# Triangular systems of four chunks solved together on VectorE, one to a partition, in an RWKV-7 recurrence with a tanh-shrink layer

## The chip, the cores and the metric

The kernel runs on one core of a Trainium2 chip. The metric is device time in microseconds (us) of one execution, and a version's time is the median of its runs. The engines named below are TensorE (PE, with PEld its weight loads), VectorE (DVE), ScalarE (ACT), GpSimd (POOL) and SyncE (SP), which issues the DMAs. Each engine takes its instructions in the order in which they were written for it.

## The reference

```python
# r, k, v, w, a, b: (4, 8, 768, 40); w lies in 0.85 .. 0.95; w_in: (320, 2048), w_out: (2048, 320)
for t in range(S):
    y[:, :, t] = np.einsum('bhd,bhde->bhe', rt, state)
    Sa = np.einsum('bhde,bhe->bhd', state, at)
    state_decay = state * wt[:, :, None, :] - np.einsum('bhd,bhe->bhde', Sa, bt)
    state = state_decay + np.einsum('bhd,bhe->bhde', vt, kt)
x = y.transpose(0, 2, 1, 3).reshape(3072, 320)
h = x @ w_in
return (h - np.tanh(h)) @ w_out
```

Everything is float32, but for the two weights, which come as float64 and are taken apart into float32 on the chip.

## The kernel before

The 768 tokens are cut into 24 chunks of 32. One chunk covers all 4 batches and 8 heads: a tile of 128 partitions holds 4 x 32 tokens, and matrices over tokens are block diagonal. Heads go in pairs, each head's 40 channels on 64 partitions. Within a chunk the recurrence is a unit lower triangular system of 32 x 32 for each batch and head, (I + N) U = -(A V + A S0), where S0 is the state that enters the chunk.

`prep(c)` does what needs no state. It loads k, b, a, r, v as `x_t`, takes the running products of the decays (`pr`, a scan), their reciprocals (`rp`), scales k, b and a, turns four of these to tokens on partitions (`p_nat`, `nat`), and forms the products (`p_prod`) of b with a (`m`, and the first `z`) and of k with a (`at`). Then comes the inverse: block sizes 2, 4, 8, 16, for each half of the heads, each a transpose (`p_flip`, line 246), a product with m (`p_g`, masked on VectorE at line 280 into `g`) and a product with z (`p_z`, subtracted on VectorE at line 285). It ends with `u0`, the inverse times `av`, and `w_`, the inverse times a (`p_w`).

`chain(c)` does what needs the state `st`: `p_u` = w times st, `ub` and `vb` (u and v spread over the batches), the new state (`p_st`), the transposes `p_s` of the old state and `p_ut` of u, the products `rv` and `ru`, the output `p_y` and `y`, and the transposes `p_x` that hand 128 tokens to the layer.

The layer runs for 256 tokens, that is, after every second chunk. It is a generator of ten pieces: eight pairs of rows of `p_h` = w_in times x with tanh and its series (ACT, POOL and DVE), then two outputs `p_o`. A call of `tick()` issues one piece. Before the change there are five ticks a chunk, four between the steps of the inverse and one in `chain`, so the ten pieces spread over two chunks. The weights are loaded and converted in 40 pieces through the scratch tiles `raw`, `wt`, `wf` (lines 159 to 174), 20 after chunk 0 and the rest after chunk 1. A scheduler sets the final order on each engine from the order of the code, so pieces of neighbouring steps interleave. All PSUM results but the layer's share five banks (`bank`); the layer has three of its own.

Of the kernel before, what the change touches and what calls it, by code (L numbers as in the profile page):

```python
# [53 lines left out]
def rwkv_shrink(ctx: ExitStack, tc: tile.TileContext, r, k, v, w, a, b, tok, dec, chan, w_in, w_out, out):  # L54
# [10 lines left out]
    assert B * L == P and DP >= D and H % 2 == 0 and NCH % 2 == 0  # L65
# [10 lines left out]
    un = chunks.enter_context(tc.tile_pool(name="un", bufs=2))  # L76
# [18 lines left out]
    # before[s, t] = 1 where s < t in one batch  # L95
# [4 lines left out]
    # pair_t[s, t] = -1 where s and t = s + 1 are a block of two  # L100
    pair_t = fixed("pair_t", [P, P], BF16)
    G.memset(pair_t, 0.0)
    v_ = pair_t.rearrange("p (j q) -> p j q", q=2)[:, :, 1]
    G.memset(v_, -1.0)
    keep(v_, Alu.is_equal, [[-2, P // 2]], 0, 1)
    # join[h][t, s] = 1 where t is in the second and s in the first half of one block of 2 h
    join = {}
    h = 2
    while h < L:
        m_ = join[h] = fixed(f"join{h}", [P, P], BF16)  # L110
        G.memset(m_, 0.0)
        v_ = m_.rearrange("p (j q) -> p j q", q=2 * h)[:, :, 0:h]
        G.memset(v_, 1.0)
        keep(v_, Alu.is_ge, [[-2 * h, P // (2 * h)], [0, h]], -h, 1)
        keep(v_, Alu.is_ge, [[2 * h, P // (2 * h)], [0, h]], 2 * h - 1, -1)
        h *= 2
    # own[p, b] = 1 where partition p is a token of batch b
# [4 lines left out]
    # half[p, e] = 1 where partition p is a channel of the pair's head e  # L122
# [4 lines left out]
    # what the scan of the decays adds: 1 before each batch's first token  # L127
# [5 lines left out]
    # of each chunk: the greatest and the least product of decays; 0, or NaN if an output isn't finite  # L133
# [6 lines left out]
    # the state, transposed: [(e, channel of k), batch, pair, e', channel of v], zero but for e = e'  # L140
    st = fixed("st", [P, B, HP, 2, DP])
    G.memset(st, 0.0)
    u_nat = [fixed(f"u_nat{i}", [P, H, DP]) for i in range(2)]
# [7 lines left out]

    def weight(dst, src, n):
        """A piece of a weight, [rows, n], into SBUF as float32."""
# [4 lines left out]
        # float64 bits: sign 1, exponent 11, fraction 52, low word first (and values in float32's range).  # L158
        raw = ff.tile([P, WP, 2], I32, name="raw", tag="raw", bufs=1)[:rows, :n]
        nc.sync.dma_start(out=raw, in_=src.bitcast(I32).rearrange("p (n two) -> p n two", two=2))  # L160
        lo, hi = raw[:, :, 0], raw[:, :, 1]
        t_ = ff.tile([P, WP], I32, name="wt", tag="wt", bufs=1)[:rows, :n]
        f_ = ff.tile([P, WP], I32, name="wf", tag="wf", bufs=1)[:rows, :n]
# [21 lines left out]
    todo = []  # L185
# [7 lines left out]
    def prep(c):  # L193
        g = {}
        v_n = g["v"] = io.tile([P, H, D], F32, name="v_n", tag="v_n")
        nc.sync.dma_start(out=v_n, in_=tok[c].rearrange("p (h d) -> p h d", h=H))
        w_t = io.tile([P, HP * B * E1], F32, name="w_t", tag="w_t", bufs=1)
        nc.sync.dma_start(out=w_t, in_=dec[c])
        x_t = io.tile([P, 5, HP, P], F32, name="x_t", tag="x_t", bufs=2)
        nc.sync.dma_start(out=x_t, in_=chan[c].rearrange("p (j q t) -> p j q t", j=5, q=HP))  # L200
        k_t, b_t, a_t, r_t, v_t = (x_t[:, j] for j in range(5))
        g["r_t"], g["v_t"] = r_t, v_t

        # the decays' running products: pr[..., i] is that of i tokens
        pr_ = sb.tile([P, HP * B, E1], F32, name="pr", tag="pr", bufs=2)
        V.tensor_tensor_scan(pr_.rearrange("p x i -> p (x i)"), w_t, reset.rearrange("p x i -> p (x i)"), 0.0,
                             Alu.mult, Alu.add)
        # (held to where quotients of them are sound: if one of them was not there, seen tells)
        V.tensor_scalar(pr_, pr_, PR_MAX, None, Alu.min, Alu.max, accum_out=seen[:, c, 0:1])
        V.tensor_scalar(pr_, pr_, PR_MIN, None, Alu.max, Alu.min, accum_out=seen[:, c, 1:2])  # L210
        rp = sb.tile([P, HP * B, L], F32, name="rp", tag="rp")
        V.reciprocal(rp, pr_[:, :, 1:])  # L212
        blk = lambda x: x.rearrange("p q (b t) -> p (q b) t", b=B)
        G.tensor_tensor(blk(k_t), blk(k_t), rp, Alu.mult)  # L214
        G.tensor_tensor(blk(b_t), blk(b_t), rp, Alu.mult)
        V.tensor_tensor(blk(a_t), blk(a_t), pr_[:, :, 0:L], Alu.mult)
        pe_t = rp.rearrange("p (q b) t -> p q (b t)", q=HP)
        G.tensor_copy(rp, pr_[:, :, 0:L])
        # the state's decay over the chunk, for both halves of a pair
        pc = g["pc"] = sb.tile([P, B, HP, 2], F32, name="pc", tag="pc", bufs=2)  # L220
# [3 lines left out]
        nat = sb.tile([P, 4, H, DP], F32, name="nat", tag="nat", bufs=2)  # L224
        g["k"], g["b"], g["a"], g["p"] = (nat[:, j] for j in range(4))
        for j, x in enumerate((k_t, b_t, a_t, pe_t)):
            p_ = bank("p_nat")
            for q in range(HP):
                T.transpose(p_[:, q * P:(q + 1) * P], x[:, q, :], ident)  # L229
            A.copy(nat[:, j].rearrange("p h d -> p (h d)"), p_)  # L230

        def prod(e, l_, r_):
            p_ = bank("p_prod")
            for q in range(HP):
                r0 = e * DP
                mm(p_[:, q * P:(q + 1) * P], l_[r0:r0 + D, q, :], r_[r0:r0 + D, q, :], q == 0)
            return p_.rearrange("p (q t) -> p q t", q=HP)
        g["prod"] = prod

        def unit(name, bufs=2):  # L240
            return un.tile([P, HP, P], F32, name=name, tag=name, bufs=bufs)

        def flip(src, dst):
            p_ = bank("p_flip")
            for q in range(HP):
                T.transpose(p_[:, q * P:(q + 1) * P], src[:, q, :], ident)  # L246
            A.copy(dst.rearrange("p q t -> p (q t)"), p_)  # L247

        g["z"], ats = [], []
        ms = []  # L250
        for e in range(2):
            m_ = unit("m")
            p_ = prod(e, b_t, a_t)
            A.copy(m_, p_)
            z = unit("z", 4)
# [9 lines left out]
        for h in range(H):  # L265
            mm(p_av[:, h * D:(h + 1) * D], ats[h % 2][:, h // 2, :], v_n[:, h, :], h == 0)
# [203 lines left out]
    while todo:  # L470
        tick()
# [57 lines left out]
```

## Time and profile before

| | us |
|---|---|
| median of 3 runs | 2021.6 |
| lowest and highest run | 1999.52 and 2028.64 |
| span of the profiled execution | 2022.6 |
| TensorE busy in it | 1836.2 |
| VectorE busy in it | 1133.3 |

The profile is of one execution. Its page gives the busy time of each engine, the chain of work that ended last, and the costliest groups of instructions. A group's row has the line, the engine and operation, the tile written and the tiles read, the shapes, the count, then the busy time in us and the mean duration of one in ns, then the idle time of the engine just ahead of it with what ended that idle time. Matrix products of float32 are two instructions each in the trace, transposes one. The mean duration of a matmul contains its pipeline, so the spacing of starts says more about throughput than the mean. A row of the timeline has the start and the length of a run of equal instructions. A window's row has its length, each engine's busy time with the number of instructions, the granted TensorE clock as a share of full speed, the share of the DMA engines and GB/s.

### The profile page before, as it was taken

Reading aid. Unit: us, or ns where it says so; the run is one execution under the profiler, and the core shown is the slowest. Engines: PE = TensorE matmul, PEld = TensorE weight load, DVE = VectorE, ACT = ScalarE, POOL = GpSimd, SP = SyncE. Lnnn points to the kernel's source line nnn. Section 1 sums busy time; section 2 is a strip of 40 time slices with the busy share of each in tenths; the row PEclk is TensorE's granted clock in tenths of the full one; section 3 lists DMA queues with packets and bytes.
Section 4 is the critical chain, followed back from the end, with each engine's and each line's share of the span. In section 5 each row is a group of like instructions: output and inputs, shape, how many; then the busy total and the mean of one; then the engine's idle time right before and its main releaser. Section 6 shows DMA issues by size and latency. Waiting matters only on the chain.

```text
span 2022.6 us, 28394 instructions
## 1 busy us (share of the span) xinstructions
PE 1836.2 (91%) x11978; PEld 1474.7 (73%) x11978; DVE 1133.3 (56%) x1887; ACT 478.0 (24%) x909; POOL 401.6 (20%) x400
## 2 busy tenths in 40 slices
PE   4878897889999999899899899899899899989998
PEld 4767676777777877777777777777777777777865
DVE  6577768667465375474375375366365457347333
ACT  1011221113132132231132132132122123123121
POOL 4011130103122032031032032032022122122012
PEclk9977879798897899998898998988978979889867
DMA  3111011110101001001001010010010000100000
GB/s 104 52 36 54 13 42 45 61 60 15 38 5 35 30 13 39 30 9 39 30 10 36 7 36 31 12 35 27 16 36 14 29 30 1 36 27 1 7 1 8
DMA packets 18916, 58.17 MB, mean 29 GB/s; under 512 B 1888, under 2 KB 8032, under 8 KB 15712
## 3 DMA queue, kind: packets, MB, share of 16 engines
q1 hardware_dynamic: 18784, 56.30, 8.4%
q8 instruction: 96, 1.57, 0.3%
q14 instruction: 36, 0.29, 0.0%
HBM read 52.36 MB, written 3.93 MB: 28 GB/s over the span
## 4 chain that ended last, share of the span: by engine, by line
PE 79%; DVE 12%; POOL 4%; issue 2%; ACT 2%; DMA 1%; SPq 0%; ACTq 0%; DVEq 0%; POOLq 0%
PE p_h L85 16%; PE p_o L85 11%; PE p_g L85 10%; PE p_z L85 9%; PE p_y L85 8%; PE p_flip L246 5%; PE p_st L85 4%; DVE rp L212 4%; PE p_u L85 3%; PE p_nat L229 3%; PE p_av L85 3%; PE p_prod L85 3%; PE p_s L325 2%; DVE g L280 2%; POOL z L257 2%
## 5 line engine op out<-in xcount | busy, mean ns | idle before, releaser
L85 PE MATMUL p_h<-xT,w 128*128 128x256 f32 (+1 forms) x1152 | 395.4, 461 | 2.9 <-DVE w L174 2.4
L85 PEld LDWEIGHTS p_h<-xT,w 128*128 128x128 f32 (+1 forms) x1152 | 206.1, 213 | 131.3 <-issue 116.1
L85 PE MATMUL p_o<-w,gt 128*128 128x320 f32 x768 | 278.3, 491 | 0.2 <-DVE w L174 0.2
L85 PEld LDWEIGHTS p_g<-t,m 128*128 128x128 f32 x1536 | 217.5, 212 | 80.6 <-ACT t L247 70.6
L85 PE MATMUL p_g<-t,m 128*128 128x128 f32 x1536 | 238.4, 304 | 35.4 <-ACT t L247 35.4
L85 PE MATMUL p_z<-z,g 128*128 128x128 f32 x1536 | 228.6, 296 | 45.3 <-DVE g L280 45.3
L85 PEld LDWEIGHTS p_z<-z,g 128*128 128x128 f32 x1536 | 206.6, 205 | 84.9 <-DVE g L280 77.1
L280 DVE TENSOR_TENSOR g<-p_g,join 128x512 f32<-128x512 f32 x192 | 132.1, 688 | 185.1 <-PE p_g L85 184.6
L247 ACT COPY t<-p_flip 128x512 f32<-128x512 f32 x192 | 112.5, 586 | 472.9 <-PE p_flip L246 469.8
L285 DVE TENSOR_TENSOR z<-z,p_z 128x512 f32<-128x512 f32 x192 | 131.3, 684 | 136.3 <-PE p_z L85 135.4
L329 POOL TENSOR_TENSOR vb<-v_n,own 128x1280 f32<-128x1280 f32 x23 | 53.8, 2340 | 665.1 <-PE p_st L85 665.1
L85 PEld LDWEIGHTS p_o<-w,gt 128*128 128x128 f32 x768 | 148.2, 214 | 49.6 <-issue 19.9
L246 PE MATMUL p_flip<-ident,z 128*128 128x128 f32 x768 | 132.0, 294 | 40.0 <-POOL z L257 40.0
L403 POOL TENSOR_SCALAR qu<-qu 128x512 f32<-128x512 f32 x96 | 63.3, 659 | 509.6 <-ACT qu L399 509.3
L246 PEld LDWEIGHTS p_flip<-ident,z 128*128 128x128 f32 x768 | 100.1, 156 | 42.7 <-POOL z L257 42.5
L404 POOL TENSOR_TENSOR qu<-qu,sq 128x512 f32<-128x512 f32 x96 | 126.6, 1318 | 7.9
L212 DVE RECIPROCAL rp<-pr 128x512 f32<-128x512 f32 x24 | 80.4, 3352 | 74.4 <-PE p_nat L229 74.4
L405 DVE SCALAR_TENSOR_TENSOR qu<-qu,sq 128x512 f32<-128x512 f32 x96 | 66.3, 690 | 92.4 <-POOL qu L404 92.4
L85 PE MATMUL p_prod<-x_t 40*128 40x128 f32 x1152 | 112.1, 289 | 1.7 <-DVE st L343 1.7
L397 ACT ACTIVATE th<-p_h 128x512 f32<-128x512 f32 x96 | 57.3, 597 | 229.9 <-PE p_h L85 229.5
L85 PEld LDWEIGHTS p_prod<-x_t 40*128 40x128 f32 x1152 | 102.7, 191 | 10.7 <-issue 6.2
L214 POOL TENSOR_TENSOR x_t<-x_t,rp 128x512 f32<-128x512 f32 x24 | 31.0, 1293 | 369.5 <-DVE rp L212 369.5
(267 smaller groups left out, 2461.2 us busy)
## 6 DMA issues: line engine op xcount, KB each, us to landing
x_t<-in_chan SPq DMA_DIRECT2D x24, 1280.0 KB
w_t<-in_dec SPq DMA_DIRECT2D x24, 264.0 KB
raw<-in_w_out SPq DMA_DIRECT2D x16, 320.0 KB
raw<-in_w_in SPq DMA_DIRECT2D x16, 256.0 KB
v_n<-in_tok SPq DMA_DIRECT2D x24, 160.0 KB
raw<-in_w_in SPq DMA_DIRECT2D x8, 128.0 KB
out<-o__2684 SPq DMA_DIRECT2D x1, 160.0 KB
out<-o__2746 SPq DMA_DIRECT2D x1, 160.0 KB
```

The source lines that it names most:

```text
L85: T.matmul(o, l_, r_, start=first, stop=last, skip_group_check=True)
L212: V.reciprocal(rp, pr_[:, :, 1:])
L229: T.transpose(p_[:, q * P:(q + 1) * P], x[:, q, :], ident)
L246: T.transpose(p_[:, q * P:(q + 1) * P], src[:, q, :], ident)
L247: A.copy(dst.rearrange("p q t -> p (q t)"), p_)
L280: V.tensor_tensor(gg, p_.rearrange("p (q t) -> p q t", q=HP), heads4(join[h_]), Alu.mult)
L285: V.tensor_tensor(z2.rearrange("p q t -> p (q t)"), z.rearrange("p q t -> p (q t)"), p2, Alu.subtract)
L329: G.tensor_tensor(vb, g["v"].rearrange("p h d -> p (h d)").unsqueeze(1).to_broadcast([P, B, DM]), own.unsqueeze(2).to_broadcast([P, B, DM] ...
L397: A.activation(t_, p_, Act.Tanh)
L403: G.tensor_scalar(q_, q_, -1.0, GAM, Alu.mult, Alu.add)
L404: G.tensor_tensor(q_, q_, s_, Alu.mult)
L405: V.scalar_tensor_tensor(q_, q_, C0, s_, Alu.add, Alu.mult)
```

## The change

`prep` becomes two functions. `first(c)` does the decays and the scaling, forms only the 32 x 32 blocks of b times a (`p_n`, `n_c`) and stores them in DRAM (`n_d`). When four chunks have done so, their 4 x 4 x 8 = 128 systems are loaded with one system to a partition (`nt`), and `invert` solves them by 31 steps of substitution, a multiply and a subtract each, on VectorE. The inverses go through DRAM (`z_d`) into two block diagonal tiles `z`. `second(c)` does the rest that needs no state, and `chain` applies the inverse to one right hand side, `rhs`, made of `at` times v and a times the state. The first four chunks are prepared and inverted before chunk 0. Later, the `first` calls of the next group stand after the first two chunks of a group, and `invert` is advanced two steps at each tick. Ticks now stand at twelve places in `second` and `chain`. The two halves of the heads alternate in `p_prod`. The scratch for the weights is now in the buffer of the layer's `gt`, in two turns. `y_t` (r and v) has one buffer, `n_c`, `nt`, `zt` and `nat` one, `x_t` and `rp` six.

```diff
+GR = 4
+NK = 6
...
+    space = ff.tile([P, 2, NF * P], I32, name="gt", tag="gt", bufs=1)
...
     def tick():
         while todo and next(todo[0], todo) is todo:
             todo.pop(0)
+        step()
+        step()
+    def step():
+        while subst and next(subst[0], subst) is subst:
+            subst.pop(0)
...
+    def first(c):
...
+        n_c = sb.tile([P, HP, 2, L], F32, name="n_c", tag="n_c")
+        p_e = [bank(f"p_n{e}") for e in range(2)]
+        for q in range(HP):
+            for b in range(B):
+                for e in range(2):
+                    r0, t0 = e * DP, b * L
+                    mm(p_e[e][t0:t0 + L, q * L:(q + 1) * L], b_t[r0:r0 + D, q, t0:t0 + L],
+                       a_t[r0:r0 + D, q, t0:t0 + L], q == 0)
+        for e in range(2):
+            A.copy(n_c[:, :, e, :], p_e[e][:, :HP * L].rearrange("p (q t) -> p q t", q=HP))
...
+        for b in range(B):
+            nc.sync.dma_start(out=n_d[c % GR, b].rearrange("h (s t) -> s h t", t=L),
+                              in_=n_c[b * L:(b + 1) * L].rearrange("p q e t -> p (q e) t"))
+    def invert(i_):
+        nt = sb.tile([P, L, L], F32, name="nt", tag="nt")
+        nc.sync.dma_start(out=nt.rearrange("p s t -> p (s t)"), in_=systems[i_].rearrange("c b h x -> (c b h) x"))
...
+        for j in range(L - 1):
+            k_, n_ = j + 1, L - 1 - j
...
+            V.tensor_tensor(t3, nt[:, j, j + 1:].unsqueeze(1).to_broadcast([P, k_, n_]),
+                            zt[:, 0:k_, j].unsqueeze(2).to_broadcast([P, k_, n_]), Alu.mult)
+            V.tensor_tensor(zt[:, 0:k_, j + 1:], zt[:, 0:k_, j + 1:], t3, Alu.subtract)
+            yield
+        z_d = inverses[i_] = dr.tile([GR, B, H, L * L], F32, name="z_d", tag="z_d", bufs=2)
+        nc.sync.dma_start(out=z_d.rearrange("c b h x -> (c b h) x"), in_=zf)
+        yield
+    def second(c, g):
...
+        y_t = io.tile([P, 2, HP, P], F32, name="y_t", tag="y_t", bufs=1)
...
+        for b in range(B):
+            nc.sync.dma_start(out=z[b * L:(b + 1) * L, :, b * L:(b + 1) * L],
+                              in_=inverses[c // GR][c % GR, b].rearrange("h (s t) -> s h t", t=L))
...
-        h_ = 2
-        while h_ < L:
...
     def chain(c, g, x_t):
+        p_r = bank("p_r")
+        for h in range(H):
+            mm(p_r[:, h * D:(h + 1) * D], g["at"][h % 2][:, h // 2, :], g["v"][:, h, :], h == 0)
         if c > 0:
             for q in range(HP):
                 for b in range(B):
+                    mm(p_r[b * L:(b + 1) * L, 2 * q * D:2 * (q + 1) * D], g["a_t"][:, q, b * L:(b + 1) * L],
+                       st[:, b, q, :, :D], False)
+        rhs = sb.tile([P, H, D], F32, name="rhs", tag="rhs")
+        A.activation(rhs.rearrange("p h d -> p (h d)"), p_r[:, :DM], Act.Copy, scale=-1.0)
+        p_u = bank("p_u")
+        for h in range(H):
+            mm(p_u[:, h * D:(h + 1) * D], g["z"][:, h, :], rhs[:, h, :], h == 0)
...
-    g = prep(0)
+    parts = [first(c) for c in range(GR)]
+    for _ in invert(0):
+        pass
     for c in range(NCH):
...
+        second(c, parts[c])
+        chain(c, parts[c], x_t)
+        if nxt < NCH and i_ < 2:
+            parts += [first(nxt + 2 * i_ + j) for j in range(2)]
+            if i_ == 1:
+                subst.append(invert(nxt // GR))
...
+        if i_ == GR - 1:
+            while subst:
+                step()
```

On TensorE before, the inverse of a chunk stands with the layer's `p_o` (or `p_h`) between its steps; this is the first part of one chunk:

```order
L85 MATMUL p_g<-t,m 128x128 x4
L85 MATMUL p_o<-w_132,gt 128x320 x2
L85 MATMUL p_z<-z,g 128x128 x4
L246 MATMUL p_flip<-ident,z 128x128 x4
L85 MATMUL p_o<-w_132,gt 128x320 x2
```

On TensorE now, this is the middle of an even chunk, ahead of the state's update (`p_st`):

```order
L88 MATMUL p_h<-xT,w_111 128x256 x14
L88 MATMUL p_r<-v_n,at 128x40
L88 MATMUL p_h<-xT,w_111 128x256 x3
L88 MATMUL p_r<-v_n,at 128x40 x7
L88 MATMUL p_r<-st,x_t 32x80 x16
L88 MATMUL p_h<-xT,w_111 128x256 x2
L88 MATMUL p_u<-rhs,z_103 128x40 x8
L330 MATMUL p_s<-ident,st 128x128 x16
```

And this is the same place in the odd chunk that follows:

```order
L88 MATMUL p_r<-v_n,at 128x40 x8
L88 MATMUL p_r<-st,x_t 32x80 x16
L88 MATMUL p_u<-rhs,z_104 128x40 x8
L330 MATMUL p_s<-ident,st 128x128 x16
L88 MATMUL p_st<-vb,nat 128x320
L88 MATMUL p_st<-ub,nat 128x320
```

The steps p_g, p_z and p_flip are gone, the layer's matmuls stand in runs in the even chunks, and none stand in the odd ones.

On VectorE now, the substitution (lines 256 and 258) stands between the layer's operations, here in the third chunk of a group:

```order
L406 TENSOR_TENSOR gt<-p_h,th 128x512
L256 TENSOR_TENSOR tmp<-nt,zt 128x175
L409 SCALAR_TENSOR_TENSOR qu<-qu,sq 128x512
L258 TENSOR_TENSOR zt<-zt,tmp 128x7x25
L410 TENSOR_TENSOR qu<-qu,p_h 128x512
L412 TENSOR_SCALAR mk<-sq 128x512
L256 TENSOR_TENSOR tmp<-nt,zt 128x192
```

Where g and z stood four times for each half of the heads in every chunk, two small operations now stand between two of the layer's.

On ScalarE now, at the head of the second chunk of a group, the copies `n_c` of two calls of `first` stand around the copies of `nat`; what an instruction waits for stands in brackets:

```order
L234 COPY n_c<-p_n_4134 128x4x32 [waits DMAHW5_49,DMAHW7_49,DMAHW0_49,PE_49]
L234 COPY n_c<-p_n_4135 128x4x32 [waits PE_49]
L282 COPY nat<-p_nat 128x512 [waits DVE_49,PE_49]
L282 COPY nat<-p_nat 128x512 [waits PE_49] x2
L234 COPY n_c<-p_n_4192 128x4x32 [waits DMAHW2_49,DMAHW1_49,DMAHW7_49,DMAHW0_49,Activation_49]
L234 COPY n_c<-p_n_4193 128x4x32
L316 ACTIVATE rhs<-p_r 128x320 [waits PE_49]
```

The third copy waits for DMAs that read the first two, and `rhs` stands behind it.

More of the change, by code (lines that the diff above doesn't have):

```diff
@@ L142, in rwkv_shrink @@
     G.memset(st, 0.0)
+    z_bufs = [fixed(f"z{i}", [P, H, P]) for i in range(2)]
+    for z_ in z_bufs:
+        G.memset(z_, 0.0)
     u_nat = [fixed(f"u_nat{i}", [P, H, DP]) for i in range(2)]
@@ new lines, in second @@
+    def second(c, g):
+        v_n = g["v"] = io.tile([P, H, D], F32, name="v_n", tag="v_n")
+        nc.sync.dma_start(out=v_n, in_=tok[c].rearrange("p (h d) -> p h d", h=H))
+        y_t = io.tile([P, 2, HP, P], F32, name="y_t", tag="y_t", bufs=1)
+        nc.sync.dma_start(out=y_t, in_=chan[c, :, 3 * HP * P:].rearrange("p (j q t) -> p j q t", j=2, q=HP))
+        g["r_t"], g["v_t"] = y_t[:, 0], y_t[:, 1]
+        z = g["z"] = z_bufs[c % len(z_bufs)]
+        for b in range(B):
+            nc.sync.dma_start(out=z[b * L:(b + 1) * L, :, b * L:(b + 1) * L],
+                              in_=inverses[c // GR][c % GR, b].rearrange("h (s t) -> s h t", t=L))
+        nat = sb.tile([P, 3, H, DP], F32, name="nat", tag="nat")
+        g["k"], g["b"], g["p"] = (nat[:, j] for j in range(3))
+        for j, x in enumerate((g["k_t"], g["b_t"], g["pe"])):
@@ L238, in prep @@
         g["prod"] = prod
[L240 to L255, printed above, removed]
-            V.tensor_tensor(z, p_, heads4(pair_t), Alu.mult)
-            G.tensor_tensor(z, z, heads4(ident), Alu.add)
-            ms.append(m_)
-            g["z"].append(z)
@@ L291, in prep @@
-        p_u = bank("p_u0")
-        for h in range(H):
-            mm(p_u[:, h * D:(h + 1) * D], g["z"][h % 2][:, h // 2, :], av[:, h, :], h == 0)
-        u0 = g["u0"] = sb.tile([P, DM], F32, name="u0", tag="u0", bufs=2)
-        A.copy(u0, p_u[:, :DM])
-        p_w = bank("p_w")
-        for h in range(H):
-            r0 = (h % 2) * DP
-            mm(p_w[r0:r0 + DP, (h // 2) * P:(h // 2 + 1) * P], g["a"][:, h, :], g["z"][h % 2][:, h // 2, :], h < 2)
-        w_ = g["w"] = sb.tile([P, HP, P], F32, name="w_", tag="w_", bufs=2)
@@ L301, in prep @@
-        A.activation(w_.rearrange("p q t -> p (q t)"), p_w, Act.Copy, scale=-1.0)
-        return g
+        g["at"] = []
+        for x in prod(g["k_t"], g["a_t"]):
+            at = un.tile([P, HP, P], F32, name="at", tag="gram")
+            V.tensor_tensor(at, x, heads4(before), Alu.mult)
+            g["at"].append(at)
+        tick()
     def chain(c, g, x_t):
@@ L334, in chain @@
             for q in range(HP):
+                tick()
                 p_ = bank("p_st")
@@ L351, in chain @@
         ru, rv = [], []
-        for e in range(2):
-            x = un.tile([P, HP, P], F32, name="rv", tag="rv")
-            V.tensor_tensor(x, g["prod"](e, g["v_t"], g["r_t"]), heads4(before), Alu.mult)
-            rv.append(x)
-        for e in range(2):
-            x = un.tile([P, HP, P], F32, name="ru", tag="ru")
-            V.tensor_tensor(x, g["prod"](e, u_t, g["r_t"]), heads4(before), Alu.mult)
-            ru.append(x)
+        for x_, l_, n_ in ((rv, g["v_t"], "rv"), (ru, u_t, "ru")):
+            for p_ in g["prod"](l_, g["r_t"]):
+                x = un.tile([P, HP, P], F32, name=n_, tag="gram")
+                V.tensor_tensor(x, p_, heads4(before), Alu.mult)
+                x_.append(x)
+            tick()
         for h in range(H):
```

119 lines of the change are left out of this document (42 added, 77 removed).

## Prediction

> **What bounds the kernel now.** I read the page's busy line and its chain of work that ended last, then the groups by shape, then windows with the granted clock, then the timeline of the stages that the change touches.
>
> ```profile
> PE 1836.2 (91%) x11978; PEld 1474.7 (73%) x11978; DVE 1133.3 (56%) x1887; ACT 478.0 (24%) x909; POOL 401.6 (20%) x400
> PE 79%; DVE 12%; POOL 4%; issue 2%; ACT 2%; DMA 1%; SPq 0%; ACTq 0%; DVEq 0%; POOLq 0%
> q1 hardware_dynamic: 18784, 56.30, 8.4%
> ```
>
> TensorE is busy 91% of the span and is 79% of the chain; VectorE is half idle. The transposes p_x close a chunk, so they date the chunks: these three close chunks 3, 7 and 23 (counted from 0).
>
> ```profile
> 368.45 0.90 PE L380 MATMUL p_x<-ident,y 128*128 128x128 f32 x3 [0.61 <-DVE y L370]
> 700.47 0.52 PE L380 MATMUL p_x<-ident,y 128*128 128x128 f32 x3
> 1944.47 0.90 PE L380 MATMUL p_x<-ident,y 128*128 128x128 f32 x3 [0.61 <-DVE y L370]
> ```
>
> Sixteen chunks, eight pairs, take 1244 us: 155.5 us a pair, each pair carrying one call of the layer. The windows (length, then busy us of PE, PEld, DVE, ACT, POOL, the granted clock, DMA) say what fills that:
>
> ```profile
> 700.47:1944.47 1244.00, 1164.08 (x8036) 941.62 (x8034) 658.66 (x998) 318.30 (x609) 250.38 (x233) 0.91 0.07 23
> 1944.47:2022.60 78.13, 71.22 (x165) 40.69 (x165) 24.86 (x47) 15.83 (x28) 17.58 (x16) 0.63 0.02 5
> 1945.00:1996.00 51.00, 50.54 (x98) 26.77 (x96) 20.60 (x38) 13.17 (x23) 15.35 (x14) 0.50 0.00 0
> ```
>
> Per pair TensorE works 145.5 us and idles 10. The last layer alone is a tail of 78 us, in which p_h runs at half clock although TensorE never idles. The clock matters elsewhere too; these windows cover the end of one chunk:
>
> ```profile
> 997.00:1000.40 3.40, 3.40 (x40) 3.28 (x40) 2.94 (x5) 0.45 (x1) 1.46 (x2) 1.00 0.00 0
> 1000.40:1003.80 3.40, 3.40 (x20) 3.40 (x20) 0.03 (x1) 0.00 (x0) 0.00 (x0) 0.57 0.00 0
> 1007.20:1010.60 3.40, 3.40 (x16) 3.36 (x17) 0.50 (x2) 1.70 (x4) 0.00 (x0) 0.50 0.87 319
> ```
>
> The clock falls while p_y (40 columns a matmul) keeps TensorE busy, and stays at 0.5 until the next chunk's transposes have run: some 10 us a chunk, costing about 5.
>
> **The change, part by part.** *Squaring removed from TensorE.* Its groups, and the same work at full clock in the timeline:
>
> ```profile
> L85 PE MATMUL p_g<-t,m 128*128 128x128 f32 x1536 | 238.4, 304 | 35.4 <-ACT t L247 35.4
> L85 PE MATMUL p_z<-z,g 128*128 128x128 f32 x1536 | 228.6, 296 | 45.3 <-DVE g L280 45.3
> L246 PE MATMUL p_flip<-ident,z 128*128 128x128 f32 x768 | 132.0, 294 | 40.0 <-POOL z L257 40.0
> L85 PE MATMUL p_prod<-x_t 40*128 40x128 f32 x1152 | 112.1, 289 | 1.7 <-DVE st L343 1.7
> L85 PE MATMUL p_w<-z,nat 128*64 128x128 f32 x384 | 37.6, 288 | 0.0
> 960.36 1.05 PE L85 MATMUL p_g<-t,m 128*128 128x128 f32 x8
> 961.25 1.24 PE L85 MATMUL p_o<-w,gt 128*128 128x320 f32 x4
> 962.33 1.05 PE L85 MATMUL p_z<-z,g 128*128 128x128 f32 x8
> 963.22 0.60 PE L246 MATMUL p_flip<-ident,z 128*128 128x128 f32 x4
> 963.66 1.24 PE L85 MATMUL p_o<-w,gt 128*128 128x320 f32 x4
> 1024.83 2.28 PE L85 MATMUL p_h<-xT,w 128*128 128x256 f32 x8
> 1945.83 50.52 PE L85 MATMUL p_h<-xT,w 128*128 128x256 f32 x96 [0.46 <-ACT xT L382]
> ```
>
> The groups together are 599 us, 25.0 a chunk, at the clock as it was. Start to start at full clock, p_g takes 0.89 us, p_z 0.89, p_flip 0.44: 2.2 us, eight times a chunk, 17.8 us. I take this lower figure, since groups overlap. With it go p_w (37.6/24 = 1.6), the transposes of a (0.44) and the product of b and a (16 instructions of 97 ns, 1.6). Together 21.4 us a chunk.
>
> *p_n added.* 64 instructions of 32x32 a chunk. Nearest below is p_u<-st, which also fills strips of 32 columns, 32 in 0.76 us or 24 ns each: 1.5 us. Nearest above is p_prod at 97 ns: 6.2 us. I take 2.0, as neighbours go to different strips. The other solve, p_u on rhs, and p_r on at and st replace p_u on av, p_av and p_u on w, count for count: nothing, in work. Net per pair: -2 x 19.4 = -39 us.
>
> ```profile
> 989.18 0.76 PE L85 MATMUL p_u<-st,w__6467 128*32 128x80 f32 x32 [0.69 <-ACT w__6467 L301]
> 989.87 1.97 PE L325 MATMUL p_s<-ident,st 128*128 128x128 f32 x16
> 991.35 1.49 DVE L332 TENSOR_TENSOR ub<-p_u,own 128x1280 f32<-128x1280 f32 x1 [0.77 <-ACT u_nat L317]
> L280 DVE TENSOR_TENSOR g<-p_g,join 128x512 f32<-128x512 f32 x192 | 132.1, 688 | 185.1 <-PE p_g L85 184.6
> L285 DVE TENSOR_TENSOR z<-z,p_z 128x512 f32<-128x512 f32 x192 | 131.3, 684 | 136.3 <-PE p_z L85 135.4
> L212 DVE RECIPROCAL rp<-pr 128x512 f32<-128x512 f32 x24 | 80.4, 3352 | 74.4 <-PE p_nat L229 74.4
> L206 DVE TENSOR_TENSOR_SCAN pr<-w_t,reset 128x528 f32<-128x528 f32 x24 | 47.9, 1997 | 33.2 <-POOL rp L218 24.4 <-POOL reset L130 8.8
> L209 DVE TENSOR_SCALAR_CACHE_REDUCE pr<-pr 128x528 f32<-128x528 f32 x24 | 16.8, 699 | 0.5
> L216 DVE TENSOR_TENSOR x_t<-x_t,pr 128x512 f32<-128x512 f32 x24 | 20.0, 834 | 0.0
> ```
>
> *Substitution on VectorE.* 684 ns for 512 elements and 1491 for 1280 give 146 ns plus 1.05 ns an element. A group of four chunks has 62 operations on 2 x 5456 elements: 9.1 + 11.5 = 20.5 us, six groups 123 us, against 263 us of g and z removed. VectorE gets lighter. The steps stand between the layer's operations, in the second half of each group, where it has time: nothing on the path, except that later operations of the chain wait a third of a us behind one.
>
> *The layer gathered in even chunks.* There are now 12 ticks a chunk, so all ten pieces fall in the first chunk of a pair and the odd chunk has no filler. Going through its chain: it waits for at (two operations of 0.68 plus hand-offs, 1.5 us), for rhs (0.6), and for y (0.6); ub's 1.49 is covered by the 16 transposes p_s, and u_t by the product of v and r. So 3 us of waits replace the 10 us of old idle time (mostly the squaring's own): -7 a pair.
>
> *p_n at the head of a chunk.* Two chunks of four begin with two p_n clusters. n_c has one buffer, so the second copy on ScalarE waits until four DMAs have read the first, and behind it stand rhs and, through the five banks, p_prod. Price: the copy, issue, and landing. The nearest row is this load of 1280 KB, issued at 1006.62 and over within the window ending 1010.60 above or just behind it, so 4 us for far more bytes:
>
> ```profile
> 1006.62 0.33 SPq L200 DMA_DIRECT2D x_t<-in_chan  x1
> ```
>
> 4 us twice in four chunks, from 0 (hidden) to 8: +4 a pair, and +2 for the time that chain operations queue. y_t has one buffer too, but its load has 20 us before v and r are used.
>
> *The clock.* p_r and p_u are now one run of 40-column matmuls and thin ones, like p_y; I count a second drop of the clock in each odd chunk (4 us) and a slower start of p_h in the even one (3 us): +7. Bounds: 0 to +30, as in the second rival. **A pair:** 155.5 - 39 - 7 + 6 + 7 = 122.5 us.
>
> *The alternating products.* The heads' two halves now alternate in p_prod. The row of p_u<-st shows neighbours in different column strips at 24 ns; no row shows different row strips. I take no gain, with up to 2 us a chunk at the low end. [...]
>
> *The start.* Four chunks must be prepared and a group inverted before chunk 0, and the first layer's gt waits for all weights, whose scratch is now that buffer. In VectorE's order the last weight operation stands in chunk 2. Ahead of it: nine preparations of 7.7 us (scan 2.0, two clamps of 0.7 and their read-outs, reciprocal 3.35, product 0.83) 69, the weights, 52 inversion pairs 36, chains 28.
>
> ```profile
> sum 600.00, DVE 100.62; mean DVE 16.77
> sum 600.00, DVE 64.66; mean DVE 10.78
> L164 DVE TENSOR_SCALAR wf<-raw x40: 264/294/1071, 13.8 to 438.9; 128x256 int32<-128x256 int32 x16, 128x320 int32<-128x320 int32 x16, 64x256 int32<-64x256 int32 x8
> 1996.40 19.75 PE L85 MATMUL p_o<-w,gt 128*128 128x320 f32 x64
> ```
>
> The first two are VectorE's busy time on tiles wf and raw; the third is in both, 40 of 0.3 us, so weights are about 152 us. Sum 285, from 9 us on at 90%: 325. Then eight layer tiles of about 4 us (p_h alone is 12 x 0.285 = 3.4), 64 p_o at 0.31, p_y: chunk 2 ends near 380. An odd chunk: the pair's 145.5 less 10 for the half clock less the layer at full clock (96 x 0.285 + 64 x 0.27 = 45) is 45 a chunk, less 19.4 is 26, plus 3 of waits and 9 for the clock: 38 us. So chunk 3 ends near 418, against 368 before. Bounds 370 to 450.
>
> **Sum.** 418 + ten pairs x 122.5 - 5 (chunk 23 updates no state) + the unchanged tail 78 = 1716 us. It is made against the profiled span of 2022.6 us, which is 1 us from the median of 2021.6.
>
> **Rivals.** *The clock stays up.* If only idle time dropped it, the old 10 us (two chunks of 5) and my 7 would go: 105 a pair, and p_h in the tail, 96 in 50.5 us, would take 27. 418 + 1050 - 5 + 55 = 1518. Speaking against it: the 51 us window at 0.50 with TensorE busy 50.54. 10%. [...]
>
> *The clock stays down.* In even chunks some 70 p_h instructions now stand together before p_r, without the p_g and p_z that ran between them. If they run as in the tail (0.526 us) rather than at 0.285, a pair pays 17 more, and up to 8 more if the odd chunk stays down: 140 to 148, so 1891 to 1971. For it: that window. Against: transposes still stand between. 18%.
>
> *The small DMAs become the bound.* n_d and z move 2 x 1024 pieces of 128 bytes a chunk, 128 per DMA engine. The queue line gives 0.084 x 16 x 2022.6 / 18784 = 145 ns a packet: 19 us a chunk, hidden. From 0.6 us a piece (77 us) they are longer than a chunk was; at 0.7 the kernel takes 24 x 90 = 2150. Nothing in the profile shows pieces that slow. 4%. *The inverse comes late* is milder: each of five groups would have to be 60 us late to cancel the gain.
>
> **How the numbers follow.** My forecast 68%, clock up 10%, clock down 18%, small DMAs 4%. The forecast's own width is 1590 to 1830 (start +-40, p_n and DMA waits +-40, clock +-60). The range 1540 to 1900 takes in half of each clock rival and leaves out 18%. Runs before spread over 1.4%, so 2% is about what can be told from no change. Faster by over 2% (below 1981): the forecast, clock up, nearly all of clock down: 0.93; within 2%: 0.03; slower: 0.04.
>
> **What would show it.** p_flip, p_g, p_z gone; TensorE busy near 1250 us; 62 operations a group at 0.18 to 0.42 us; odd chunks 32 to 45 us and even ones 75 to 95; chunk 3 ending at 380 to 450. Wrong if p_r or p_u waits for z in steady chunks, if p_h is at 0.5 through whole even chunks, or if ScalarE waits over 8 us at n_c.

## The result and the profile after

The changed kernel takes 1586.5 us (median of four runs, 1565.8 to 1596.4) against 2012.9 us for the kernel before (four runs, 1999.5 to 2028.6). The ratio is 0.781, with a 95% interval of 0.773 to 0.789. The forecast was 1716 us in a range of 1540 to 1900. The ratio is that of the faster runs, for the changed kernel 1565.8 and 1577.0 us (mean 1571.4); the other two took 1596 us, the profiled execution (1596.0 us, span 1594.3) among them, so its durations are compared with each other below and small differences between two kernels are not read from it.

The page of the changed kernel: busy time of the engines, the chain that ended last, and the DMA queue.

```profile
PE 1356.3 (85%) x8810; PEld 1021.4 (64%) x8810; DVE 932.1 (58%) x1804; ACT 315.9 (20%) x645; POOL 356.8 (22%) x347
PE 65%; DVE 26%; POOL 3%; issue 2%; ACT 2%; DMA 1%; SPq 0%; ACTq 0%; DVEq 0%; POOLq 0%
q1 hardware_dynamic: 76192, 68.90, 15.4%
```

TensorE has 3168 matmul instructions fewer and is still the bound, but VectorE's part of the chain has doubled. The queue moves four times the packets in 15.4% of its time, that is 52 ns a packet (0.154 x 16 x 1594.3 / 76192): the small pieces are hidden.

Windows of the changed kernel, up to the end of chunk 3, to the end of chunk 23, and the tail (length, busy us of PE, PEld, DVE, ACT, POOL, clock, DMA):

```profile
359.73:1516.05 1156.32, 1087.83 (x7149) 825.31 (x7149) 624.95 (x1092) 261.32 (x532) 261.45 (x240) 0.77 0.13 35
1516.05:1594.30 78.25, 71.06 (x165) 40.60 (x165) 24.96 (x47) 15.83 (x28) 17.57 (x16) 0.63 0.02 5
```

Chunk 3 ends at 359.7 us instead of 368.5, ten pairs take 115.6 us each instead of 157.6 (1944.47 less 368.45, by ten), and the tail is unchanged. So nearly all of the gain lies in the steady pairs. This is the same stretch of the kernel before:

```profile
368.45:1944.47 1576.02, 1478.12 (x10081) 1192.91 (x10081) 853.56 (x1329) 398.50 (x762) 316.91 (x293) 0.90 0.08 25
```

A pair loses 39.0 us of TensorE's busy time (147.8 less 108.8) and 2.9 us of its idle time (9.8 less 6.9), although the granted clock fell from 0.90 to 0.77. Two even chunks in the same place of their groups, chunk 8 and chunk 12, are the most telling rows of this profile:

```profile
600.30:691.29 90.99, 90.24 (x387) 62.99 (x387) 41.76 (x66) 20.26 (x38) 22.40 (x21) 0.69 0.09 25
844.36:912.44 68.08, 66.80 (x388) 47.87 (x388) 44.22 (x66) 19.82 (x38) 22.69 (x21) 0.95 0.12 33
```

The same instructions in the same order took 91.0 us in one and 68.1 in the other. TensorE is busy throughout both; the granted clock is 0.69 in one and 0.95 in the other. Their timelines, at the same place, show where:

```profile
607.99 1.11 PE L281 MATMUL p_nat<-ident,x_t 128*128 128x128 f32 x4
608.90 6.22 PE L88 MATMUL p_h<-xT,w 128*128 128x256 f32 x12
615.05 1.12 PE L281 MATMUL p_nat<-ident,rp 128*128 128x128 f32 x4
...
850.48 0.66 PE L281 MATMUL p_nat<-ident,x_t 128*128 128x128 f32 x4
850.97 3.34 PE L88 MATMUL p_h<-xT,w 128*128 128x256 f32 x12
```

Twelve p_h take 6.2 us or 3.3. Where the clock was down when p_h began, p_h did not soon bring it up again: of the ten steady even chunks four (6, 8, 14 and 16) took 91 to 98 us at a clock of 0.67 to 0.69, with 72 to 74 of their 96 p_h at half clock; six took 67 to 79 at 0.89 or more, with 18 or fewer.

The odd chunks were to have 3 us of waits. This is chunk 5, TensorE and VectorE, and the window of the chunk (an idle time and what ended it stand in brackets):

```profile
432.63 1.41 PE L88 MATMUL p_prod<-x_t 40*128 40x128 f32 x16
436.74 3.75 PE L88 MATMUL p_r<-v_n,at 128*128 128x40 f32 x16 [2.70 <-issue]
442.28 3.64 PE L88 MATMUL p_u<-rhs,z 128*128 128x40 f32 x16 [0.56 <-ACT rhs L316]
457.68 0.41 PE L88 MATMUL p_y<-nat,rv 128*128 128x40 f32 x2 [1.57 <-DVE rv L361]
...
432.74 3.35 DVE L213 RECIPROCAL rp<-pr 128x512 f32<-128x512 f32 x1 [4.39 <-PE p_nat L281]
436.01 1.22 DVE L298 TENSOR_TENSOR at<-p_prod,before 128x512 f32<-128x512 f32 x2
```

The windows of the whole chunk and of the 14 us from the idle time on:

```profile
427.81:465.65 37.84, 32.21 (x356) 28.84 (x356) 16.09 (x26) 6.21 (x16) 5.64 (x5) 0.68 0.22 58
434.00:448.00 14.00, 10.75 (x76) 10.29 (x76) 4.72 (x4) 1.97 (x6) 1.78 (x2) 0.56 0.30 84
```

TensorE idles 5.6 us of 37.8. The longest wait, 2.7 us ahead of p_r, has no releaser in its row ("issue"), but the times tell it: p_r begins as the first half of `at` is done, and before `at` on VectorE stands the reciprocal that `first` does for a later chunk, 3.35 us long. The clock is 0.56 over these 14 us, and p_r, p_u and p_s run at half speed (p_u takes 3.64 us, against 1.98 in chunk 10 at full clock).

### The profile page after: what moved, and what is told of

The parts are those of the page before. It is cut to its first block, busy times and chain, and to the rows that moved or that the text cites. A ratio compares the mean times of both kernels' runs of the same rounds, so it can differ in the third digit from the quotient of the medians.

```text
span 1594.3 us, 21763 instructions
## 1 busy us (share of the span) xinstructions
PE 1356.3 (85%) x8810; PEld 1021.4 (64%) x8810; DVE 932.1 (58%) x1804; ACT 315.9 (20%) x645; POOL 356.8 (22%) x347
## 2 busy tenths in 40 slices
DMA packets 76297, 70.34 MB, mean 44 GB/s; under 512 B 54688, under 2 KB 60832, under 8 KB 76192
## 3 DMA queue, kind: packets, MB, share of 16 engines
q1 hardware_dynamic: 76192, 68.90, 15.4%
## 4 chain that ended last, share of the span: by engine, by line
PE 65%; DVE 26%; POOL 3%; issue 2%; ACT 2%; DMA 1%; SPq 0%; ACTq 0%; DVEq 0%; POOLq 0%
PE p_h L88 21%; PE p_o L88 9%; PE p_y L88 9%; PE p_r L88 5%; PE p_st L88 5%; PE p_u L88 4%; PE p_s L330 4%; DVE tmp L256 3%; DVE zt L258 3%; PE p_nat L281 3%; DVE rp L213 3%; PE p_prod L88 2%; DVE rv L361 2%; DVE pr L207 1%; PE p_x L384 1%
## 5 line engine op out<-in xcount | busy, mean ns | idle before, releaser
L88 PE MATMUL p_o<-w,gt 128*128 128x320 f32 x768 | 216.7, 441 | 2.7 <-DVE gt L413 2.7
L406 DVE TENSOR_TENSOR gt<-p_h,th 128x512 f32<-128x512 f32 x96 | 65.6, 684 | 120.3 <-ACT sq L402 120.3
L88 PE MATMUL p_u<-rhs,z 128*128 128x40 f32 x384 | 76.8, 382 | 56.2 <-DMA z<-z_d 47.3
L88 PEld LDWEIGHTS p_u<-rhs,z 128*128 128x128 f32 x384 | 75.3, 298 | 61.7 <-issue 47.4
L88 PE MATMUL p_r<-v_n,at 128*128 128x40 f32 x384 | 76.7, 368 | 39.0 <-issue 32.0
L88 PEld LDWEIGHTS p_r<-v_n,at 128*128 128x128 f32 x384 | 74.0, 283 | 48.4 <-issue 38.3
L334 POOL TENSOR_TENSOR vb<-v_n,own 128x1280 f32<-128x1280 f32 x23 | 54.7, 2377 | 180.0 <-PE p_st L88 98.1
L88 PE MATMUL p_y<-nat,rv 128*128 128x40 f32 x384 | 62.3, 319 | 38.4 <-DVE rv L361 36.9
L88 PEld LDWEIGHTS p_y<-nat,rv 128*128 128x128 f32 x384 | 56.3, 226 | 45.2 <-DVE rv L361 44.0
L413 DVE COPY_PREDICATED gt<-mk,qu 128x512 f32<-128x512 uint8 x96 | 84.6, 881 | 0.4
L256 DVE TENSOR_TENSOR tmp<-nt,zt 128x31 f32<-128x31 f32 (+15 forms) x186 | 74.4, 400 | 1.9
```

The source lines that it names most:

```text
L88: T.matmul(o, l_, r_, start=first, stop=last, skip_group_check=True)
L256: V.tensor_tensor(t3, nt[:, j, j + 1:].unsqueeze(1).to_broadcast([P, k_, n_]), zt[:, 0:k_, j].unsqueeze(2).to_broadcast([P, k_, n_]), Alu. ...
L334: G.tensor_tensor(vb, g["v"].rearrange("p h d -> p (h d)").unsqueeze(1).to_broadcast([P, B, DM]), own.unsqueeze(2).to_broadcast([P, B, DM] ...
L406: V.tensor_tensor(o_, p_, t_, Alu.subtract)
L413: V.copy_predicated(o_, m_, q_)
```

## The experiments

**The clock.** From the trace of the changed kernel I added up, for each stretch of 3.41 us (the 71 changes of the granted clock in this trace lie whole multiples of 3.41 us apart), the time in which columns stream, weighted by the rows and columns of the array that a matmul uses. A column takes about 1.7 ns at half clock (16 p_s of 128 columns in chunk 5: 0.216 us each) and half that at full clock (0.111 us each in chunk 10). Of 35 rises 32 followed a stretch with 0.75 or more of the array at work; of 185 stretches that stayed down 184 had less; all 36 falls followed stretches below 0.38, and no stretch that stayed up had less. My estimate from this one trace is that the clock goes by the share of the array at work. How long TensorE is busy does not tell it: in the tail 96 p_h, one after the other, took 50.5 us, all at a clock of 0.50. Four kernels test what counts as work. The first fills the third piece of the contraction, 64 channels, with zeros to 128:

```diff
+    xts = [fixed(f"xT{i}", [P, len(KT), 2 * P]) for i in range(2)]
+    for t_ in (w1, *xts):
+        G.memset(t_[KT[-1][1]:, len(KT) - 1, :], 0.0)
...
-                    mm(p_[:, i * 2 * P:(i + 1) * 2 * P], w1[:n, k_, (f + i) * P:(f + i + 1) * P], x_t[:n, k_, :],
+                    mm(p_[:, i * 2 * P:(i + 1) * 2 * P], w1[:, k_, (f + i) * P:(f + i + 1) * P], x_t[:, k_, :],
```

> The changed kernel, with the third contraction piece of p_h filled from 64 to 128 rows by zeros; the instructions and their columns stay as they are. Theory A: the granted clock goes by the share of the array's cells that work in a window of 3.4 us, rises from about 0.75 of them and falls below about 0.38; p_h with rows 128, 128 and 64 reaches 0.70 and so stays at half clock, with 128 rows it reaches 0.83. Then p_h rises within two windows wherever it stands, the tail falls from 78 to about 55 us, the ten even chunks from 809 to about 700 us in all, and the time to about 1430 us. Theory B: the clock goes by how long TensorE is busy or idle, whatever the rows: 1565 to 1600 us, the tail stays at 78.

Measured: 1447.9 us (1446.7 to 1452.6), 0.723 of the kernel before (0.718 to 0.728). Steady part, tail, and chunk 8, the place shown above at 91.0 us:

```profile
346.04:1392.05 1046.01, 948.22 (x7149) 792.81 (x7149) 629.41 (x1092) 259.95 (x532) 264.39 (x240) 0.84 0.14 39
1392.05:1445.20 53.15, 42.71 (x165) 31.61 (x165) 28.32 (x47) 15.84 (x28) 15.23 (x16) 0.92 0.03 8
563.55:629.95 66.40, 63.84 (x388) 52.51 (x388) 43.52 (x66) 19.82 (x38) 22.66 (x21) 0.91 0.12 34
```

Its timeline in the same chunk:

```profile
572.58 2.76 PE L88 MATMUL p_h<-xT,w 128*128 128x256 f32 x12
```

The tail fell from 78 to 53 us and every even chunk lies between 64 and 77. Theory B falls. The spread of the runs fell too, from 2% to 0.4%. Part of the gain is not the clock: even at full clock twelve p_h now take 2.8 us instead of 3.3. The next kernel cuts the 320 channels otherwise:

```diff
-    KT = [(i, min(P, DM - i)) for i in range(0, DM, P)]
+    KT = [(0, P), (P, 96), (224, 96)]
```

> The changed kernel, with the 320 channels cut as 128, 96 and 96 in place of 128, 128 and 64. Theory A: the mean of the rows is the same, the share of the array is 0.70 as before, and nothing changes: 1560 to 1600 us, tail 78, p_h near 0.52 us each in the tail. Theory C: it is the short piece of 64 rows in itself that holds the clock down; then this does what the filling does: about 1430 us, tail 55.

Measured: 1463.7 us in a single run, tail 51 us, p_h in the tail twelve in 2.83 us:

```profile
1427.17 2.83 PE L88 MATMUL p_h<-xT,w 128*128 128x256 f32 x12 [0.63 <-DVE qu L410]
```

So it is the piece of 64 rows that holds p_h down, as theory C had it: with it the tail is 78 us, with the piece filled 53, and with two pieces of 96 rows 51. Theory A's expectation of no change failed; it kept the spacing of the old pieces. In the tail of the changed kernel, at half clock, pieces of 128 rows start 0.427 us apart and pieces of 64 rows 0.56 to 0.59, so that p_h filled 0.65 to 0.71 of the array where it had it to itself. Twelve p_h took 2.83 us in the tail with pieces of 96 rows as with filled ones; if pieces of 96 rows also start 0.427 us apart at half clock, which no row here shows, p_h fills 0.83 of the array (320 of 384 rows), an estimate from these spacings, and that is above the 0.75 of theory A. Whether the fewer rows count, or the gaps that the slower pieces of 64 rows leave, these runs do not separate.

The third kernel also lets the products with 40 columns stream 64 (the rows of `p_r`, `p_u` and `p_y` become 64 wide; this is one of the lines):

```diff
-            mm(p_y[:, h * D:(h + 1) * D], rv[h % 2][:, h // 2, :], g["k"][:, h, :D], h == 0)
+            mm(p_y[:, h * DP:(h + 1) * DP], rv[h % 2][:, h // 2, :], g["k"][:, h, :], h == 0)
```

> As the first, and the products with 40 columns (p_r from v, p_u, p_y) stream 64 columns into 64 wide places, of which 24 are not used. At full clock one of 40 columns keeps the array working 0.30 of the time, below the 0.38 at which theory A lets the clock fall; with 64 it is 0.48. Theory A: the clock stays at 1.0 through most of p_u, p_s and p_y; odd chunks fall from 36 to about 28 us and the time to about 1300 us. Theory B: more columns only cost time where the clock is down: 1565 to 1620 us.

Measured: 1428.5 us (1423.8 to 1430.4), ratio 0.712 (0.707 to 0.717). The expected 1300 was missed. Where VectorE has nothing to do for a later group, in chunk 21, the edit does what was expected. The kernel with p_h filled alone:

```profile
1272.51:1302.98 30.47, 28.19 (x228) 24.85 (x228) 10.26 (x19) 5.34 (x12) 2.32 (x1) 0.72 0.11 28
```

And this one:

```profile
1268.31:1291.47 23.16, 20.90 (x227) 18.13 (x228) 10.26 (x19) 5.15 (x12) 2.32 (x1) 1.00 0.15 36
```

In chunk 5 nothing is won (37.9 us at a clock of 0.74), since there the clock is down behind the idle time ahead of p_r, with 64 columns as with 40: 1.4 us of work in the 4 us around it, and then 14 us at 0.51.

```profile
411.00:415.00 4.00, 1.41 (x17) 1.18 (x17) 4.00 (x3) 1.12 (x4) 0.00 (x0) 1.00 0.18 28
415.00:429.00 14.00, 13.38 (x84) 12.32 (x85) 3.26 (x3) 2.57 (x6) 3.47 (x3) 0.51 0.32 85
```

The fourth is the kernel before with the same two edits.

> The kernel before, with the same two edits: p_h on 128 rows, and p_av, u0 and p_y on 64 columns. It tells what the change is worth when the clock stays up in both. Theory A: mean clock from 0.88 to 0.95 or more, 2013 to about 1870 us; with 1300 for the changed kernel the ratio would be 0.70, against 0.78 measured, so the change lost about a third of its gain to the clock. Theory B: 2000 to 2040 us.

Measured: 1865.4 us (1860.9 to 1871.1), 0.931 of the kernel before (0.925 to 0.938), with the clock at 0.96 in the steady part:

```profile
349.70:1810.20 1460.50, 1340.32 (x10078) 1133.08 (x10076) 869.88 (x1327) 392.97 (x762) 319.78 (x293) 0.96 0.08 27
```

With both edits in both kernels a pair falls from 146.0 to 103.3 us, by 42.7; without them from 157.6 to 115.6, by 42.0. My expectation that the change had lost a third of its gain to the clock was wrong: the edits are worth as much in either kernel (143 us before, against 2008.6, and 143 after, against 1571.4).

**The layer gathered in even chunks.** The layer is called at every second tick (the tail as before), so that its pieces spread over both chunks:

```diff
+        turn_[0] += 1
+        if turn_[0] % 2 == 0 or turn_[1]:
+            while todo and next(todo[0], todo) is todo:
+                todo.pop(0)
```

> The changed kernel with the layer advanced at every second tick, so that its ten pieces spread over both chunks of a pair as before the change; nothing padded. The prediction put the waits of an odd chunk without filler at 3 us. Theory D: in odd chunks VectorE's work for the next group (a reciprocal of 3.4 us ahead of at, a scan and a clamp ahead of rv) makes TensorE idle some 6 us, and each idle stretch also drops the clock for about 14 us of work, so that the gathering costs 10 to 15 us a pair: spread out, 1450 to 1530 us. Rival: the gathering costs no more than the 3 us: 1550 to 1600 us.

Measured: 1517.7 us (1513.2 to 1525.7), ratio 0.765 (0.759 to 0.770): the gathering costs 54 us (against 1571.4), pairs of the profiled executions are 109.6 us instead of 115.6. With the two edits on p_h and the columns:

> The padded and widened kernel (1428 us, 103 us a pair) with the layer spread in the same way. Theory D: the idle stretches of the odd chunks are filled and the clock stays up in p_r, p_u and p_y: pairs of 88 to 95 us and about 1320 us. Rival: the odd chunks lose their time to something else (the chain of dependences itself): 1400 to 1430 us.

Measured: 1334.0 us (1331.9 to 1335.4), ratio 0.673 (0.670 to 0.676), pairs of 94.9 us. Theory D has the time right in both, but not the price of 10 to 15 us a pair: it is 6.0 and 8.4. The steady parts with the two edits, gathered and then spread:

```profile
342.99:1376.28 1033.29, 924.99 (x7149) 771.93 (x7149) 639.02 (x1092) 260.11 (x532) 264.69 (x240) 0.87 0.14 39
331.20:1280.60 949.40, 878.17 (x7149) 729.88 (x7149) 629.07 (x1092) 262.41 (x532) 262.88 (x240) 0.91 0.16 43
```

TensorE's idle time falls from 10.8 to 7.1 us a pair, so 3.7 of the 8.4 us; the rest is busy time, at a clock of 0.91 instead of 0.87. Without the two edits idle time falls only from 6.9 to 5.7 us a pair: most of the 6.0 us is busy time there, at a clock of 0.81 instead of 0.77.

**The substitution.** First the changed kernel itself, with all steps but the first left out:

```diff
+            if j == 0:
+                V.tensor_tensor(t3, nt[:, j, j + 1:].unsqueeze(1).to_broadcast([P, k_, n_]),
+                                zt[:, 0:k_, j].unsqueeze(2).to_broadcast([P, k_, n_]), Alu.mult)
+                V.tensor_tensor(zt[:, 0:k_, j + 1:], zt[:, 0:k_, j + 1:], t3, Alu.subtract)
```

> The changed kernel without 30 of the 31 steps of the substitution, so what it computes is not the reference; loads, stores and everything else stand. The prediction: the 20 us of the first group go, since chunk 0 waits for them, and nothing in the steady part, where they stand between the layer's operations: 1555 to 1580 us. Rival: the steps hold up the chain's own operations on VectorE in half of the chunks: below 1530 us.

Measured: 1486.6 us in a single run, the rival's number, but not by its mechanism. Against the profiled execution of the changed kernel, chunk 5 ended 31 us earlier (435 instead of 466); of the other 79 us most is the clock, since of the later even chunks one took over 90 us and not four. On so uneven a base 30 us cannot be priced, so it was repeated where the clock is held up:

> The padded, widened and spread kernel (1334 us) without 30 of the 31 steps of the substitution, so what it computes is not the reference; here the clock is held up and no longer blurs the price. The prediction: about 25 us at the start and nothing in the steady part: pairs stay near 95 us, 1300 to 1315 us. Rival: the steps stand ahead of the chain's own operations on VectorE and TensorE waits for these: pairs of 90 us or less, below 1285 us.

Measured: 1291.1 us (1286.6 to 1293.9), 43 less than with the steps, between the two expectations. Chunk 5 ends at 402.3 instead of 430.6, so 28 us go up to there, which holds the steps of the first two groups; from there to chunk 23 it is 838.3 against 850.0 us, 1.3 us a pair. The steady steps are nearly hidden, not quite.

> The padded, widened and spread kernel with the substitution of the later five groups on GpSimd (28% busy) in place of VectorE (71%); the first group's stays on VectorE. If the steps hold up the chain's operations on VectorE, pairs fall from 95 to about 91 us and the time to 1290 us or less. If they stand in idle time there, as the prediction has it, 1315 to 1335 us; more than 1345 us if GpSimd's own work for the layer and the chain (qu, vb, x_t) is held up instead.

Measured: 1410.2 us (1408.1 to 1411.6), 76 slower. GpSimd takes 0.56 and 0.61 us for an operation where VectorE took 0.39 (143.28 us for 372 in the changed kernel), and what waits is VectorE, for the layer's `qu` (119 us, against 14 in the kernel it was made from); TensorE then waits for `rv` three times as long as there (104 against 35 us). The groups on GpSimd:

```profile
L264 POOL TENSOR_TENSOR zt<-zt,tmp 128x31 f32<-128x31 f32 (+15 forms) x155 | 95.0, 613 | 10.8
L262 POOL TENSOR_TENSOR tmp<-nt,zt 128x31 f32<-128x31 f32 (+15 forms) x155 | 86.4, 558 | 14.0 <-DMA nt<-n_d 2.9
```

And who waited for whom in the steady part (us in total, times, the longest):

```profile
DVE qu L418 <- POOL qu L417: 119.0, 34, 15.7
PE p_y L88 <- DVE rv L370: 104.2, 26, 16.0
```

**The alternating products.** The loops over the halves and the pairs of heads in `prod` change places.

> The changed kernel with the products of the two halves of the heads one after the other, as before the change, not in turns. The prediction took no gain from the turns: 1565 to 1600 us, and 97 ns from start to start in p_prod as now. Rival, two products in different halves of the rows run at the same time: at full clock 16 instructions take 1.0 us in turns and would take 1.6 us so, 48 of them a chunk: 1.8 us more in each of 24 chunks, 1610 to 1640 us.

Measured: 1517.5 us in a single run, faster, which neither side gave a reason for: one slow even chunk instead of four. Again with the clock held up:

> The padded, widened and spread kernel with the two halves of the heads one after the other in p_prod. The prediction took no gain from the turns: 1325 to 1345 us. Rival, they run at the same time: 62 ns from start to start in turns against about 90 ns so, 48 instructions a chunk: 1.3 us more in 24 chunks, 1355 to 1375 us.

Measured: 1327.5 us (1326.2 to 1338.1), ratio 0.662 (0.656 to 0.669), not slower than the 1334.0 in turns. The group of `p_prod` on k and a is 42.5 us of busy time so, and 28.2 in turns. One after the other:

```profile
L88 PE MATMUL p_prod<-x_t 40*128 40x128 f32 x384 | 42.5, 291 | 0.0
```

In turns:

```profile
L88 PE MATMUL p_prod<-x_t 40*128 40x128 f32 x384 | 28.2, 286 | 0.0
```

So the turns do make these products a third shorter (all three groups of `p_prod`: 98.1 instead of 138.1 us), and the time does not follow. The steady part one after the other, to be read beside 949.40 and 878.17 above:

```profile
330.87:1275.11 944.24, 893.09 (x7149) 753.76 (x7149) 626.68 (x1092) 262.43 (x532) 262.17 (x240) 0.91 0.16 43
```

In turns TensorE is busy 15 us less and idle 20 us more, and 13 us of the latter are p_y waiting for `rv` (35.1 us against 22.4): what the turns save is waited for again, since VectorE has to mask the products first.

## Why the prediction was right or wrong, point by point

The direction and the range were right, and the time 130 us too high. Against the profiled span, the start was 58 us too high, the steady part 64 (1220 us against 1156), the tail right. A pair was to fall by 33 us (39 and 7 to the good, 6 and 7 to the bad) from 155.5; it fell by 42.0 from 157.6, so the pair of 115.6 us is 7 below the forecast 122.5: 9 by the fall, less 2 by the base.

**p_n, mis-sized in both its terms: six of these nine us.** Its 1536 instructions are 20.3 us, 0.85 us a chunk instead of 2.0: 13 ns each, below even the neighbour that was taken as the lower bound. That makes 2.3 us a pair. The wait at `n_c` for the DMAs, priced at 4 us a pair, is 2.0 us in the whole run:

```profile
L88 PE MATMUL p_n<-x_t 40*32 40x32 f32 x1536 | 20.3, 244 | 41.4 <-POOL x_t L215 41.4
L234 ACT COPY n_c<-p_n 128x128 f32<-128x128 f32 x48 | 10.5, 274 | 46.7 <-PE p_n L88 42.7 <-DMA n_d<-n_c 2.0 <-ACT xT L388 1.9
```

If the squaring was worth its 21.4 us a chunk (no run takes it out alone), 41 of the 42 us are then told. For the other three terms (7 less idle time, 2 more of queueing, 7 more for the clock: 2 us worse) that leaves 1 us better. That these three came out together is luck: idle time fell by 2.9 us with waits of every kind in it, which leaves 2 us for the clock where 7 were priced.

**The gathered layer: the step that failed.** "So 3 us of waits replace the 10 us of old idle time": the list of waits held the chain's own operations and left out what `first` puts ahead of them on VectorE. Chunk 5 idles 5.6 us, and with the idle stretch ahead of p_r the clock is down for some 14 us (0.56 from 434 to 448 us). All in all the idle time of a pair went from 9.8 to 6.9 us, not from 10 to 3. Spreading the layer gave back 6.0 us a pair, and 8.4 with the two edits (103.3 to 94.9).

**The clock.** It was to cost 7 us a pair more than before. The two edits give back 12.3 us a pair after the change (115.6 less 103.3) and 11.6 before it (157.6 less 146.0), so what they cure was there in either kernel (some 4.6 us of each, by the twelve p_h at full clock, is p_h being shorter and not the clock). They leave a clock of 0.87 against 0.96; spreading the layer brings it to 0.91, and the rest is not told apart. Both clock rivals were put as all or nothing. Bulk p_h at half clock came true in four even chunks of ten, and where it came it cost 23 us (91.0 less 68.1), more than the 17 given. The rival in which only idle time drops the clock is excluded by the first two experiments: p_h without idle time stayed down with a piece of 64 rows (in the tail of 78 us 96 p_h in 50.5, all at half clock) and came up without (the first 36 in 9.99 us in the tail of 53, in 8.06 in the tail of 51). The sign named for a wrong prediction, "p_h is at 0.5 through whole even chunks", was seen in those four for three quarters of their p_h.

**The start.** Chunk 3 ended at 360, not 418. The sum "285, from 9 us on at 90%" took durations of VectorE's instructions as if they stood end to end. They overlap by some 80 ns, so that 276 us of durations up to the last weight are 233 us of busy time, as the starts in the changed kernel show:

```profile
263.17 0.32 DVE L168 TENSOR_SCALAR gt<-gt 128x320 int32<-128x320 int32 x1
263.40 0.32 DVE L160 TENSOR_SCALAR gt<-gt 128x320 int32<-128x320 int32 x1
263.64 0.48 DVE L169 SCALAR_TENSOR_TENSOR w<-gt 128x320 f32<-128x320 f32 x1
264.04 0.48 DVE L161 TENSOR_TENSOR gt<-gt 128x320 int32<-128x320 int32 x1
```

0.32 us start 0.235 apart, 0.48 start 0.40 apart. VectorE was busy 233 us up to the last weight at 269 us, where the forecast had 285 and 325; here is the window up to there:

```profile
0.00:268.90 268.90, 114.14 (x1098) 96.58 (x1098) 233.11 (x575) 21.93 (x53) 57.23 (x72) 0.80 0.33 97
```

The rest of the step held: chunk 2 ended 55 us after the last weight, as the 380 less 325 said.

**The substitution.** It was sized at 20.5 us a group; its 62 operations are 22.9 us in the first group, 20.8 in the second and 24.9 in a later one (99.55 us in four). On the path it was to cost its own 20 at the start and after that nothing but short waits; the runs gave 28 up to the end of chunk 5, the second group's steps included, and 1.3 a pair. VectorE's windows for the tile `tmp`:

```profile
0.00:131.04 131.04, 22.94 (x62) 0.98 0.38 116
131.04:359.73 228.69, 20.79 (x62) 0.65 0.22 61
359.73:1516.05 1156.32, 99.55 (x248) 0.77 0.13 35
```

**The alternating products.** "No gain taken" was right in time, though the products did get shorter. The group on k and a gives a factor of 1.5 in busy time (42.5 to 28.2), all three give 1.4 (138.1 to 98.1, that is 1.7 us a chunk), and the runs give nothing. The up to 2 us a chunk put at the low end had no run behind it; the runs show 1.7 in busy time and none in the kernel's time.

**What was to show it.** p_g, p_z and p_flip are gone and the tail is 78 us. Odd chunks took 25 to 39 us and even ones 67 to 98, both wider than said: the even ones by the clock, of the odd ones the last three took 25 to 32, with some 2 us of idle time instead of 3 to 6. TensorE's busy time is 1356, not 1250; the prediction gives no working for the 1250, and its own 19.4 us a chunk would have left 1371 (1836.2 less 465.6). Busy time also moves with the clock (twelve p_h are 3.3 or 6.2 us), so it is a poor measure of work removed. p_u waited for z once, 47 us at the very start, and never after. The small DMAs stayed hidden.

## What to carry to other kernels

Work off VectorE's order by starts, not by durations, and list everything that stands ahead of a chain's operation there, also what belongs to a later group. Before counting instructions saved, look at the clock in the place where the remaining ones run: here filling a contraction piece from 64 to 128 rows with zeros, streaming 64 columns for 40, and spreading independent work over the waits took the changed kernel from 1586 to 1334 us, more than half of what the change itself gained. A price that is smaller than the clock's own swings is measured on a kernel in which these have been removed.

## What the runs showed that was not expected

In p_h a contraction piece of 64 rows was slower than one of 128: at full clock twelve p_h took 3.3 us with it and 2.8 us filled. With it TensorE also stayed at half clock though it hardly idled: for 72 to 74 of 96 p_h in four even chunks, and for all 96 in the tail of 78 us, which became 53. Pieces of 96 rows behaved as full ones in the tail (twelve p_h in 2.83 us with either).

The runs of the changed kernel spread over 2%, those of the kernels in which p_h was filled over 0.3 to 0.9%. The same instructions took 68 or 91 us within one execution.
